# Attention with a normalised output, then a gated convolution network: whole-batch loads, quadrant matmuls and a norm factor spread through DRAM

## The chip, the cores and the metric

The kernel runs on one core of one Trainium2 chip. The metric is the device time of one execution in microseconds, as the median of repeated runs. The engines named below are TensorE (PE, with its weight loads shown apart as PEld), VectorE (DVE), ScalarE (ACT), GpSimd (POOL) and SyncE (SP); transfers run on 16 DMA engines, and in the kernel before all of them are issued from POOL.

## The reference

```
kv  = einsum('bhsd,bhse->bhde', k, v)          # B=8, H=8, S=576, D=64
o   = einsum('bhsd,bhde->bhse', q, kv)
rms = sqrt(mean(o*o, axis=-1) + 1e-6)
x   = (o / rms * g_norm)  -> (B, S, H*D = 512)
h   = relu(x @ w_in)                           # 512 -> 1024
c   = conv_w[0]*h[s-1] + conv_w[1]*h[s] + conv_w[2]*h[s+1]
out = (h * sigmoid(c)) @ w_out                 # 1024 -> 512, float32
```

All inputs are float32 in DRAM; both kernels compute in bfloat16 on the PE and accumulate in float32.

## The kernel before

The attention part runs per batch and per pair of heads (8 x 4 = 32 passes). A pass loads its own slices of k, v and q with nine DMAs from POOL, which also cast to bfloat16 (L163 to L179). The rows they fetch are 64 numbers long. Ten matmuls build the two 64x64 products k'v (L187), and ACT copies them into a block-diagonal 128x128 tile (L191). Five PE transposes turn q (L196), each copied out by ACT (L198). The 576 positions are then treated as a piece of 512 and a piece of 64: the product q*kv (L202), its square on ACT (L205), a matmul with a block of ones that sums the squares over each head and spreads the sum over the head's 64 rows (L208), Ln and Exp on ACT for the inverse root (L211, L213), and one DVE operation that multiplies the product, still in PSUM, by the factor and by `g_norm` into `xT` (L216). Each of these PSUM tiles has one buffer, so the next piece's L202 waits for L216.

The feed-forward part runs per batch. For each of 8 blocks of 128 of the 1024 inner features: matmuls with `w_in` (L230), Relu on ACT (L236), and three DVE operations for the three taps (L240, L241, L245). Then one Sigmoid over the whole batch (L251), one DVE product (L252), 40 matmuls with `w_out` (L257), five DVE copies out of PSUM (L264) and five output DMAs from POOL (L265).

A scheduler in the framework orders each engine's instructions, so the attention of later batches stands between the feed-forward work of earlier ones; within an engine the order is then fixed, and an instruction that waits holds up all that follow on its engine. ACT has one table of functions loaded at a time, and the compiler puts an ACT_TABLE_LOAD wherever the next function is not in it. The weights come first of all on POOL's queue, the 24 small columns of `conv_w` among them (L125), and only then the first batch's k and v.

## Time and profile before

| | |
|---|---|
| time, median of 3 runs | 528.26 us (525.47 to 528.58) |
| span of the profiled execution | 525.6 us |
| ACT busy | 376.4 us (72%) |
| PE busy | 296.3 us (56%), pipelined matmuls with modelled ends |
| POOL busy | 245.9 us (47%) |
| DVE busy | 203.6 us (39%) |
| DMA queue of POOL | 120192 packets, 27.82 MB, 50.0% of 16 engines' span |

The profile is one execution. Busy time counts the stretch in which an engine has an instruction in work. The chain of waits follows the work that ended last back through what released it. The granted TensorE clock is given as a share of 2.4 GHz and stands at 1.00 or 0.50 in any short stretch, so a mean between them is a mixture.

### The profile page before, as it was taken

The numbers are of one execution on the slowest core, as the hardware profiler recorded it, in microseconds if no ns is written. First come the engines' busy times: TensorE is split into PE (matmuls) and PEld (weight loads), VectorE is DVE, ScalarE is ACT, GpSimd is POOL, SyncE is SP. The second block draws the span as 40 slices with busy tenths as digits, with TensorE's granted clock in tenths as the row PEclk, the third lists the DMA queues.
The fourth block names the chain that finished last, engine by engine and source line by source line (L and its number), as shares of the span: only waits on it lengthen the run. The fifth ranks groups of instructions, "written<-read, shape, count | busy, mean of one in ns | idle before, by whom it ended". The sixth has DMA issues, their size and how long they took to land.

```text
span 525.6 us, 4567 instructions
## 1 busy us (share of the span) xinstructions
PE 296.3 (56%) x1414; PEld 129.9 (25%) x1440; DVE 203.6 (39%) x321; ACT 376.4 (72%) x687; POOL 245.9 (47%) x372
## 2 busy tenths in 40 slices
PE   0033346653766663676646756676655765686816
PEld 0011123321322321232212323232222222232302
DVE  4000103442215545223443344523434325768652
ACT  0028888789898888888898779977899788525130
POOL 7999854455676542665435554465533000020202
...
GB/s 305 15 68 70 65 36 34 34 41 40 46 60 98 47 35 23 66 68 60 32 34 56 75 64 35 22 69 81 54 22 24 60 30 2 0 91 1 90 0 90
DMA packets 120216, 28.11 MB, mean 53 GB/s; under 512 B 116864, under 2 KB 116864, under 8 KB 120192
## 3 DMA queue, kind: packets, MB, share of 16 engines
q0 software_dynamic: 120192, 27.82, 50.0%
...
## 4 chain that ended last, share of the span: by engine, by line
ACT 57%; PE 18%; issue 14%; POOL 5%; DVE 3%; DMA 2%; POOLq 0%
ACT L213 15%; ACT L211 14%; PE o_psum L257 6%; ACT rms_sb L211 6%; PE h_psum L230 5%; ACT rms_sb L213 5%; ACT conv_all L251 5%; ACT qT_sb L198 4%; ACT h_all L236 3%; PE ot_psum L202 3%; PE qT_psum L196 2%; POOL conv_w L125 2%; ACT sq_sb L205 2%; DVE xT L216 2%; ACT kv_sb L191 2%
## 5 line engine op out<-in xcount | busy, mean ns | idle before, releaser
L230 PE MATMUL h_psum<-xT,w_in 128*128 128x64 bf16 (+1 forms) x497 | 118.8, 372 | 39.7 <-ACT h_all L236 38.3
L216 DVE SCALAR_TENSOR_TENSOR xT<-ot_psum,g_norm_sbuf,rms_sb 128x512 bf16<-128x512 f32 x64 | 33.1, 517 | 224.1 <-ACT rms_sb L213 224.1
L257 PE MATMUL o_psum<-w_out,hg_all 128*128 128x512 bf16 (+1 forms) x309 | 101.5, 461 | 14.0 <-DVE hg_all L252 13.2
L163 POOL DMA_DIRECT2D k_sb<-in_k_dram x64 | 48.2, 757 | 110.2 <-PE qT_psum L196 77.6
L196 PE MATMUL qT_psum<-ident,q_sb 128*128 128x128 bf16 (+1 forms) x160 | 41.7, 260 | 77.5 <-ACT qT_sb L198 74.1
L213 ACT ACT_TABLE_LOAD x64 | 82.1, 1283 | 1.1
L211 ACT ACT_TABLE_LOAD x64 | 82.1, 1283 | 1.1
L236 ACT ACTIVATE h_all<-h_psum 128x512 bf16<-128x512 f32 (+1 forms) x128 | 48.4, 407 | 41.8 <-PE h_psum L230 38.7
L265 POOL DMA_DIRECT2D out_dram<-o_sb x40 | 22.9, 576 | 115.3 <-DVE o_sb L264 110.4
L230 PEld LDWEIGHTS <-w_in 128*128 128x128 bf16 x512 | 43.8, 118 | 111.0 <-issue 101.7
L174 POOL DMA_DIRECT2D q_sb<-in_q_dram x64 | 49.4, 782 | 46.3 <-PE qT_psum L196 33.8
L187 PE MATMUL kv_psum<-v_sb,k_sb 128*64 128x64 bf16 (+1 forms) x320 | 35.2, 230 | 56.2 <-DMA v_sb<-in_v_dram 31.2
L257 PEld LDWEIGHTS <-hg_all 128*128 128x128 bf16 (+1 forms) x320 | 32.5, 114 | 93.2 <-issue 46.6
L198 ACT ACTIVATE qT_sb<-qT_psum 128x128 bf16<-128x128 bf16 (+1 forms) x160 | 41.9, 262 | 16.5 <-PE qT_psum L196 14.2
L245 DVE SCALAR_TENSOR_TENSOR conv_all<-h_all,conv_w,conv_all 128x575 bf16<-128x575 bf16 x64 | 51.2, 815 | 0.7
L241 DVE SCALAR_TENSOR_TENSOR conv_all<-h_all,conv_w,conv_all 128x575 bf16<-128x575 bf16 x64 | 51.1, 813 | 0.9
L205 ACT ACTIVATE sq_sb<-ot_psum 128x512 bf16<-128x512 f32 x64 | 26.2, 409 | 34.4 <-PE ot_psum L202 32.1
L187 PEld LDWEIGHTS <-k_sb 128*64 128x64 bf16 (+1 forms) x320 | 26.5, 131 | 92.6 <-issue 59.2
L163 POOL DMA_DIRECT2D v_sb<-in_v_dram x64 | 48.2, 758 | 0.3 <-issue 0.2
L264 DVE COPY o_sb<-o_psum 128x512 f32<-128x512 f32 (+1 forms) x40 | 27.5, 688 | 51.9 <-PE o_psum L257 43.6
L202 PE MATMUL ot_psum<-qT_sb,kv_sb 128*128 128x512 bf16 x64 | 25.6, 401 | 22.0 <-DVE xT L216 21.2
L191 ACT ACTIVATE kv_sb<-kv_psum 64x64 bf16<-64x64 f32 x64 | 13.6, 212 | 30.5 <-PE kv_psum L187 29.7
...
## 6 DMA issues: line engine op xcount, KB each, us to landing
out_dram<-o_sb POOLq DMA_DIRECT2D x32, 256.0 KB, 2.4
k_sb<-in_k_dram POOLq DMA_DIRECT2D x64, 64.0 KB, 2.8
v_sb<-in_v_dram POOLq DMA_DIRECT2D x64, 64.0 KB, 2.8
q_sb<-in_q_dram POOLq DMA_DIRECT2D x64, 64.0 KB, 2.7
...
w_out_tmp<-in_moe_w_out_dram POOLq DMA_DIRECT2D x8, 256.0 KB, 6.7
...
```

Source lines behind the costliest of these rows:

```text
L163: nc.gpsimd.dma_start(out=dst[:, :nfull, r], in_=src[b, h0 + hi, :nfull * P, :].rearrange("(p si) d -> p si d", si=nfull, p=P),)
L174: nc.gpsimd.dma_start(out=q_sb[:, :nfull, r], in_=q[b, h0 + hi, :nfull * P, :].rearrange("(si p) d -> p si d", si=nfull, p=P),)
L187: nc.tensor.matmul(kv_psum[r, r], k_sb[:sc, si, r], v_sb[:sc, si, r], start=(si == 0), stop=(si == len(s_chunks) - 1),)
L196: nc.tensor.transpose(qT_psum[:, :sc], q_sb[:sc, si, :], ident128[:sc, :sc])
L198: nc.scalar.activation(qT_sb[:, s0:s0 + sc], qT_psum[:, :sc], AX.Copy)
L211: nc.scalar.activation(rms_sb[:, :nc_], sos_psum[:, :nc_], AX.Ln, bias=eps_sbuf, scale=1.0 / D)
L213: nc.scalar.activation(rms_sb[:, :nc_], rms_sb[:, :nc_], AX.Exp, scale=-0.5)
L230: nc.tensor.matmul(h_psum[:, :], w_in_tiles[ki][:, fi * P:(fi + 1) * P], x_T[ki][:, n0:n0 + nc_], start=(ki == 0), stop=(ki == n_hd - 1),)
L236: nc.scalar.activation(h_sb[:, n0:n0 + nc_], h_psum, AX.Relu)
L241: nc.vector.scalar_tensor_tensor(conv_sb[:, 1:S], h_sb[:, 0:S - 1], cw[:, 0:1], conv_sb[:, 1:S], op0=AL.mult, op1=AL.add,)
L245: nc.vector.scalar_tensor_tensor(conv_sb[:, 0:S - 1], h_sb[:, 1:S], cw[:, 2:3], conv_sb[:, 0:S - 1], op0=AL.mult, op1=AL.add,)
L257: nc.tensor.matmul(o_psum[:sc, :], hg_all[:, fi, s0:s0 + sc], w_out_tiles[fi], start=(fi == 0), stop=(fi == n_ff - 1),)
```

## The change

The file is written anew around the same mathematics.

**Loads.** k, v and q of one whole batch are loaded with one casting DMA each from POOL (batch 0 in two halves). A row is now 6 consecutive positions of one head, 384 numbers (1536 bytes in DRAM). Output DMAs, `w_in`, `g_norm` and `conv_w` go through SP; `conv_w` comes in one DMA and is turned by one PE transpose; `g_norm` is folded into `w_in`.

**Attention.** Positions are kept in the order of residue modulo 6, in two halves ("parities") of 288. A transpose turns 128 columns (two residues of one head), so even residues land on partitions 0 to 63 and odd ones on 64 to 127; DVE copies 576 columns at once (L214). The product q*kv is four matmuls on the four 64x64 quadrants of the array, two heads by two parities, 288 columns each (L267). It is computed twice: once for the squares (L222), and again when the factor is there (L279). Sums of squares of a whole group of batches gather in one PSUM tile of 128 rows (L231); one Ln and one Exp per group (L246, L247) give all factors, which SP writes to DRAM (L249) and reads back with eight broadcasting DMAs, each into 64 partitions (L254).

**Feed-forward.** Chunks of 288 or 384 columns in place of 512 and 64. A tap is one DVE multiplication per tap and feature block (L311, three in place of one) and six additions per two blocks (L315, L316), all bfloat16; Sigmoid and product go over two blocks at once. Output copies are two thirds on ACT, one third on DVE.

**Order.** The batches form five groups, (0), (1,2), (3,4), (5,6), (7). In each stage `interleave` mixes the first feed-forward half of group s, the second half of group s-1 and the attention of group s+1, by weights. The framework's scheduler then orders each engine.

```diff
+GROUPS = ((0,), (1, 2), (3, 4), (5, 6), (7,))
...
+                nc.gpsimd.dma_start(
+                    out=qkv[name, b][:, i * hs:(i + 1) * hs, :],
+                    in_=src[b, i * hs:(i + 1) * hs].rearrange("h (p r) d -> p h (r d)", r=R),
                 )
...
+        def kv_unit(bi, b):
+            k_sb, v_sb = qkv["k", b], qkv["v", b]
+            ps = ps_kq.tile([P, n_hd, D], FP32, name="kv_ps", tag="kq")
+            for hp in range(n_hd):
+                for r in range(R):
+                    for i in range(2):
+                        nc.tensor.matmul(
+                            ps[i * D:(i + 1) * D, hp, :],
+                            k_sb[:, 2 * hp + i, r * D:(r + 1) * D],
+                            v_sb[:, 2 * hp + i, r * D:(r + 1) * D],
+                            start=(r == 0), stop=(r == R - 1))
...
+        def sq_unit(bi, t):
+            ps = out_mm(g, bi, t)
+            sq = attn.tile([P, 2, HS], BF16, name="sq", bufs=5)
+            nc.scalar.activation(sq, ps[:, :, :HS], AX.Square)
...
+        def norm_unit():
+            rs = attn.tile([P, HS], FP32, name="rs")
+            nc.scalar.preload_act_table_set("natural_log_exp_and_others")
+            nc.scalar.activation(rs, g.ss, AX.Ln, bias=eps_sb, scale=1.0 / D)
+            nc.scalar.activation(rs, rs, AX.Exp, scale=-0.5)
+            scr = dram.tile([P, HS], FP32, name="scr")
+            nc.sync.dma_start(out=scr, in_=rs)
+            g.rb = bcast.tile([P, n_hd, 2 * g.G, HS], FP32, name="rb", padded_shape=[P, n_hd, 4, HS])
+            for t in range(n_hd):
+                row = scr[t * SM:t * SM + 4 * g.G, :].rearrange("(c i) n -> i c n", i=2)
+                for i in range(2):
+                    nc.sync.dma_start(
+                        out=g.rb[i * D:(i + 1) * D, t, :, :],
+                        in_=row[i:i + 1].to_broadcast([D, 2 * g.G, HS]))
...
+        ps = ps_ot.tile([P, 2, 512], FP32, name="ot_ps")
+        for i in range(2):
+            for e in range(2):
+                es = slice(e * D, (e + 1) * D)
+                nc.tensor.matmul(
+                    ps[i * D:(i + 1) * D, e, :HS],
+                    g.kv[bi][es, t, i, :], g.qT[bi][es, 2 * t + i, :],
+                    start=True, stop=True)
...
+        def x_unit(bi, t):
+            ps = out_mm(g, bi, t)
+            nc.vector.tensor_mul(
+                g.xT[:, t, bi * S:(bi + 1) * S].rearrange("p (e n) -> p e n", n=HS),
+                ps[:, :, :HS], g.rb[:, t, 2 * bi:2 * bi + 2, :])
...
+                for j in range(3):
+                    col = j * n_ff + f0 + f
+                    nc.vector.tensor_scalar_mul(taps[j][:, f, :], g.h[:, f0 + f, :], cw[:, col:col + 1])
+            v = [t.rearrange("p f (b n) -> p (f b) n", n=S) for t in taps]
+            for at, n, prev in NEIGHBOURS:
+                here, there = slice(at, at + n), slice(prev, prev + n)
+                nc.vector.tensor_add(v[1][:, :, here], v[1][:, :, here], v[0][:, :, there])
+                nc.vector.tensor_add(v[1][:, :, there], v[1][:, :, there], v[2][:, :, here])
+            nc.scalar.activation(taps[1], taps[1], AX.Sigmoid)
...
+    for s in range(ng + 1):
+        a = []
+        if s + 1 < ng:
+            for b in (groups[s + 2].bs if s + 2 < ng else ()):
+                load(b)
+            a = attn_a(groups[s + 1]) + [(4.0, lambda: None)] + attn_b(groups[s + 1])
+        m1 = mm1(groups[s]) if s < ng else []
+        m2 = mm2(groups[s - 1]) if s > 0 else []
+        interleave(m1, m2, a)
```

On ACT, in the first pass of the kernel before (`rms_sb` is the factor, `qT_sb` and `sq_sb` as above; L211 and L213 are Ln and Exp):

```order
L205 ACTIVATE sq_sb<-ot_psum 128x512
L211 ACT_TABLE_LOAD
L211 ACTIVATE rms_sb<-sos_psum,eps_sbuf 128x512
L213 ACT_TABLE_LOAD
L213 ACTIVATE rms_sb<-rms_sb 128x512
L198 ACTIVATE qT_sb<-qT_psum 128x128 x3
L205 ACTIVATE sq_sb<-ot_psum 128x64
```

On ACT of the changed kernel, in the stage that runs the feed-forward of batches 1 and 2 and the attention of batches 3 and 4 (`rs` is the factor of the group, `h` the Relu output, `tap_` the convolution sum that Sigmoid takes):

```order
L317 ACTIVATE tap_1150<-tap_1150 128x2304
L246 ACT_TABLE_LOAD
L246 ACTIVATE rs<-ss_ps,eps_sb 128x288
L303 ACTIVATE h<-h_ps 128x384
L247 ACT_TABLE_LOAD
L247 ACTIVATE rs<-rs 128x288
L303 ACTIVATE h<-h_ps 128x384 x6
L317 ACT_TABLE_LOAD
```

Before, a pair of table loads stands at each of 64 pieces; now one Ln and one Exp serve a group, with three loads around them, and 15 loads stand in the whole program.

On SP of the changed kernel, for the same group (`scr` is the DRAM tile, `rb` the spread factor, `out_dram` the output):

```order
L350 DMA out_dram<-o_sb 32x512
L249 DMA scr<-rs 128x288
L350 DMA out_dram<-o_sb 64x512 x2
L254 DMA rb<-scr 64x4x288 x8
L350 DMA out_dram<-o_sb 32x512
L350 DMA out_dram<-o_sb 96x512 x2
```

Before, SP issues nothing and the factor never leaves SBUF; now a write and eight reads stand between the Exp and its use, and outputs queue with them.

On DVE of the changed kernel, at the first use of a spread factor by this group (`xT<-ot_ps,rb` is the product of L279; the `tap_` and `h` rows are the convolution of batches 1 and 2):

```order
L315 TENSOR_TENSOR tap_1396<-tap_1396,tap_1395 128x4x288
L316 TENSOR_TENSOR tap_1396<-tap_1396,tap_1397 128x4x288
L319 TENSOR_TENSOR h<-h,tap_1283 128x2304
L279 TENSOR_TENSOR xT<-ot_ps,rb 128x576
L315 TENSOR_TENSOR tap_1396<-tap_1396,tap_1395 128x4x192
L316 TENSOR_TENSOR tap_1396<-tap_1396,tap_1397 128x4x192
```

On DVE before, `xT` (L216) waits for ACT alone; now the first L279 of a group waits for DMAs, in the middle of the last convolution unit of the group before it, whose remaining additions stand behind it.

On PE before, ahead of the first sum of squares (`sos_psum`); the `kv_psum` rows belong to the next pair of heads:

```order
L202 MATMUL ot_psum<-qT_sb,kv_sb 128x512
L187 LDWEIGHTS k_sb
L187 MATMUL kv_psum<-v_sb,k_sb 64x64
L230 LDWEIGHTS w_in_84
L230 MATMUL h_psum<-xT_0_178,w_in_84 128x64
L187 LDWEIGHTS k_sb
L187 MATMUL kv_psum<-v_sb,k_sb 64x64
L208 LDWEIGHTS ones_165
L208 MATMUL sos_psum<-sq_sb,ones_165 128x512
```

On PE of the changed kernel, ahead of the first norm (`ss_ps` gathers the squares of batch 0, `kv_ps` is the k'v product of batch 1):

```order
L231 MATMUL ss_ps<-sq,sel 32x288
L191 LDWEIGHTS k_sb
L191 MATMUL kv_ps<-v_sb,k_sb 64x64
...
L191 MATMUL kv_ps<-v_sb,k_sb 64x64
L231 LDWEIGHTS sel
L231 MATMUL ss_ps<-sq,sel 32x288
```

Before, two matmuls of the next pair of heads stand between a product and its sum; now the last five matmuls of batch 0's sum stand behind 39 matmuls of batch 1's k'v, and so behind the loads of the whole of batch 1's k and v.

## Rows read from the trace of the kernel before

**Rows 1.** The page, part 1: busy us (share of the span) and instructions.

```profile
span 525.6 us, 4567 instructions
...
PE 296.3 (56%) x1414; PEld 129.9 (25%) x1440; DVE 203.6 (39%) x321; ACT 376.4 (72%) x687; POOL 245.9 (47%) x372
```

**Rows 2.** The page, part 4: the chain that ended last, by engine and by line.

```profile
ACT 57%; PE 18%; issue 14%; POOL 5%; DVE 3%; DMA 2%; POOLq 0%
ACT L213 15%; ACT L211 14%; PE o_psum L257 6%; ACT rms_sb L211 6%; PE h_psum L230 5%; ACT rms_sb L213 5%; ACT conv_all L251 5%; ACT qT_sb L198 4%; ACT h_all L236 3%; PE ot_psum L202 3%; PE qT_psum L196 2%; POOL conv_w L125 2%; ACT sq_sb L205 2%; DVE xT L216 2%; ACT kv_sb L191 2%
```

**Rows 3.** Groups by line and shape, ACT: count, busy us, mean ns, idle before.

```profile
L211 ACT ACT_TABLE_LOAD x64 | 82.1, 1283 | 1.1
L213 ACT ACT_TABLE_LOAD x64 | 82.1, 1283 | 1.1
L236 ACT ACTIVATE h_all<-h_psum 128x512 bf16<-128x512 f32 x64 | 38.0, 594 | 20.7 <-PE h_psum L230 17.6 <-PE sos_psum L208 1.9 <-PE ot_psum L202 1.1
...
L251 ACT ACTIVATE conv_all<-conv_all 128x4608 bf16<-128x4608 bf16 x8 | 32.3, 4043 | 3.0 <-DVE conv_all L245 2.9
L211 ACT ACTIVATE rms_sb<-sos_psum,eps_sbuf 128x512 f32<-128x512 f32 x32 | 22.0, 687 | 0.5
...
L236 ACT ACTIVATE h_all<-h_psum 128x64 bf16<-128x64 f32 x64 | 14.1, 220 | 21.1 <-PE h_psum L230 21.1
```

**Rows 4.** Groups by line and shape, DVE.

```profile
L245 DVE SCALAR_TENSOR_TENSOR conv_all<-h_all,conv_w,conv_all 128x575 bf16<-128x575 bf16 x64 | 51.2, 815 | 0.7
...
L216 DVE SCALAR_TENSOR_TENSOR xT<-ot_psum,g_norm_sbuf,rms_sb 128x512 bf16<-128x512 f32 x32 | 24.0, 750 | 117.2 <-ACT rms_sb L213 117.1
L240 DVE TENSOR_SCALAR conv_all<-h_all,conv_w 128x576 bf16<-128x576 bf16 x64 | 22.9, 370 | 4.8 <-ACT h_all L236 4.4
L264 DVE COPY o_sb<-o_psum 128x512 f32<-128x512 f32 x32 | 22.1, 689 | 45.1 <-PE o_psum L257 36.7 <-remote 5.9 <-DMA k_sb<-in_k_dram 1.5
L252 DVE TENSOR_TENSOR hg_all<-h_all,conv_all 128x4608 bf16<-128x4608 bf16 x8 | 20.5, 2558 | 26.8 <-ACT conv_all L251 26.8
...
L119 DVE CAST w_out<-w_out_tmp 128x512 bf16<-128x512 f32 x8 | 3.4, 427 | 1.8 <-DMA w_out_tmp<-in_moe_w_out_dram 1.8
L112 DVE CAST w_in<-w_in_tmp 128x1024 bf16<-128x1024 f32 x4 | 2.8, 694 | 6.0 <-DMA w_in_tmp<-in_moe_w_in_dram 6.0
```

**Rows 5.** Windows: us, busy of PE, PEld, DVE, ACT, POOL, clock, DMA share, GB/s.

```profile
36.00:468.00 432.00, 260.52 (x1236) 113.94 (x1259) 162.76 (x255) 357.94 (x657) 208.82 (x304) 0.72 0.54 48
380.00:390.00 10.00, 7.74 (x36) 3.42 (x36) 5.02 (x8) 8.35 (x18) 4.24 (x6) 0.50 0.47 30
455.60:459.00 3.40, 3.35 (x8) 1.19 (x9) 1.91 (x3) 0.43 (x1) 0.00 (x0) 0.50 0.00 0
462.00:466.20 4.20, 4.15 (x20) 1.68 (x18) 1.38 (x2) 0.00 (x0) 1.61 (x3) 1.00 0.34 132
```

**Rows 6.** Timeline, PE, k'v matmuls: start us, us, [idle before].

```profile
30.36 0.37 PE L187 MATMUL kv_psum<-v_sb,k_sb 128*64 128x64 bf16 x4 [30.36 <-DMA v_sb<-in_v_dram]
...
66.06 0.61 PE L187 MATMUL kv_psum<-v_sb,k_sb 128*64 128x64 bf16 x5
```

**Rows 7.** Groups by line and shape, PE: matmuls of 128 and 64 columns.

```profile
L196 PE MATMUL qT_psum<-ident,q_sb 128*128 128x128 bf16 x128 | 34.5, 269 | 73.7 <-ACT qT_sb L198 70.3 <-DMA q_sb<-in_q_dram 3.2
...
L187 PE MATMUL kv_psum<-v_sb,k_sb 128*64 128x64 bf16 x256 | 23.7, 226 | 55.4 <-DMA v_sb<-in_v_dram 30.4 <-ACT kv_sb L191 23.3 <-DMA q_sb<-in_q_dram 1.5
```

**Rows 8.** The page, parts 2, 3 and 6: rate per slice, queue, issues (us to landing).

```profile
GB/s 305 15 68 70 65 36 34 34 41 40 46 60 98 47 35 23 66 68 60 32 34 56 75 64 35 22 69 81 54 22 24 60 30 2 0 91 1 90 0 90
...
q0 software_dynamic: 120192, 27.82, 50.0%
...
out_dram<-o_sb POOLq DMA_DIRECT2D x32, 256.0 KB, 2.4
k_sb<-in_k_dram POOLq DMA_DIRECT2D x64, 64.0 KB, 2.8
```

More of the change, by code (lines that the diff above doesn't have):

```diff
@@ L55, with interleave @@
 AL = mybir.AluOpType
+PSUM = bass.MemoryType.PSUM
+DRAM = bass.MemoryType.DRAM
+GROUPS = ((0,), (1, 2), (3, 4), (5, 6), (7,))
+def interleave(*lists):
+    keyed = []
+    for n, units in enumerate(lists):
+        total = float(sum(w for w, _ in units)) or 1.0
+        at = 0.0
+        for m, (w, fn) in enumerate(units):
+            keyed.append(((at + 0.5 * w) / total, n, m, fn))
+            at += w
+    for _, _, _, fn in sorted(keyed, key=lambda x: x[:3]):
+        fn()
 @with_exitstack
@@ new lines @@
+    SM = 32
+    pool = lambda name, bufs, **kw: ctx.enter_context(tc.tile_pool(name=name, bufs=bufs, **kw))
+    consts = pool("consts", 1)
+    loads = pool("loads", 2)
+    attn = pool("attn", 2)
+    big = pool("big", 2)
+    bcast = pool("bcast", 1)
+    conv = pool("conv", 2)
+    outp = pool("outp", 3)
+    dram = pool("dram", 2, space=DRAM)
+    ps_h = pool("ps_h", 2, space=PSUM)
+    ps_o = pool("ps_o", 2, space=PSUM)
+    ps_ot = pool("ps_ot", 1, space=PSUM)
+    ps_ss = pool("ps_ss", 1, space=PSUM)
@@ new lines @@
+    ps_kq = pool("ps_kq", 1, space=PSUM)
+    from concourse.masks import make_identity
+    ident = consts.tile([P, P], BF16, name="ident")
+    make_identity(nc, ident)
+    ident32 = consts.tile([3 * n_ff, 3 * n_ff], FP32, name="ident32")
+    make_identity(nc, ident32)
+    eps_sb = consts.tile([P, 1], FP32, name="eps_sb")
+    nc.vector.memset(eps_sb, eps)
+    sel = consts.tile([P, 4, SM], BF16, name="sel")
+    nc.vector.memset(sel, 0.0)
+    for c in range(4):
+        nc.vector.memset(sel[:D, c, 2 * c:2 * c + 1], 1.0)
+        nc.vector.memset(sel[D:, c, 2 * c + 1:2 * c + 2], 1.0)
@@ L168, with load @@
+    qkv = {}
+    def load(b, parts=1):
+        hs = H // parts
+        for i in range(parts):
+            for name, src in (("k", k), ("v", v), ("q", q)):
+                if i == 0:
+                    qkv[name, b] = loads.tile([PS, H, R * D], BF16, name=name + "_sb")
                 nc.gpsimd.dma_start(
-                    out=dst[:sc, nfull, :].rearrange("p (h d) -> p h d", h=2, d=D),
-                    in_=src[b, h0:h0 + 2, s0:s0 + sc, :].rearrange("h p d -> p h d"),
-                )
@@ L172 @@
-            for hi in range(2):
-                r = slice(hi * D, hi * D + D)
-                nc.gpsimd.dma_start(
-                    out=q_sb[:, :nfull, r],
-                    in_=q[b, h0 + hi, :nfull * P, :].rearrange(
-                        "(si p) d -> p si d", si=nfull, p=P),
-                )
-            nc.gpsimd.dma_start(
-                out=q_sb[:sc, nfull, :].rearrange("p (h d) -> p h d", h=2, d=D),
-                in_=q[b, h0:h0 + 2, s0:s0 + sc, :].rearrange("h p d -> p h d"),
-            )
@@ L183 @@
-            kv_psum = attn_psum.tile([P, P], FP32, name="kv_psum")
-            for hi in range(2):
-                r = slice(hi * D, hi * D + D)
-                for si, (s0, sc) in enumerate(s_chunks):
-                    nc.tensor.matmul(
-                        kv_psum[r, r], k_sb[:sc, si, r], v_sb[:sc, si, r],
-                        start=(si == 0), stop=(si == len(s_chunks) - 1),
-                    )
-                nc.scalar.activation(kv_sb[r, r], kv_psum[r, r], AX.Copy)
-            qT_sb = attn.tile([P, S], BF16, name="qT_sb")
@@ new lines @@
+    w_stage = []
+    for t in range(n_hd):
+        st = loads.tile([P, D_ff], FP32, name="w_stage")
+        nc.sync.dma_start(out=st, in_=moe_w_in[t * P:(t + 1) * P, :])
+        nc.vector.tensor_scalar_mul(w_in_sb[:, t, :], st, g_sb[:, 0:1])
+    cw_ps = ps_ss.tile([P, 3 * n_ff], FP32, name="cw_ps", tag="ss")
+    nc.tensor.transpose(cw_ps, cw_rows, ident32)
+    cw = consts.tile([P, 3 * n_ff], FP32, name="cw")
+    nc.vector.tensor_copy(cw, cw_ps)
+    load(1)
+    w_out_sb = consts.tile([P, n_ff, D_model], BF16, name="w_out_sb")
```

271 lines of the change are left out of this document (128 added, 143 removed).

## The prediction

> **What bounds the kernel now.** I read the page's engine shares first, then the chain that ended last, then the groups by line and shape, and last a few windows and the timeline. The shares [rows 1] put ACT in front with 376.4 us of 525.6; PE is 120 us behind by pipelined, modelled busy time, DVE has 203.6. The chain [rows 2] is 57% ACT, and its two largest lines, L213 and L211 with 15% and 14%, are not Exp and Ln but the table loads ahead of them: 64 each, 1283 ns every time [rows 3], 164.2 us together. From 36 to 468 us ACT is busy 357.94 of 432 us [rows 5], 83%, at a mean PE clock of 0.72: a kernel bound by one engine, with some loss at hand-overs. The first matmul waits for v until 30.36 us [rows 6], because POOL issues the weights first.
>
> **The sum, engine by engine.** The rewrite leaves little in place, so I price each engine's whole new work from rows, then the start, the end and the loss between them.
>
> ACT. Relu costs 594 ns for 512 columns and 220 for 64 [rows 3], so 0.835 ns a column: 72 of 384 columns at 0.49 and 32 of 288 at 0.41 make 48 us. 32 squares of 576 at 0.65: 21. Sigmoid at 4043/4608 = 0.877 ns a column: 12 of 2304 and 8 of 1152, 35. 32 copies of k'v (256 columns) at 0.38: 12. 25 output copies at 0.594: 15. Five Ln and Exp of 288 at up to 0.5 each: 5. Table loads stand 15 times in the new order, 19 us, for the 128 of those two rows. Together 155 us, so 221 of 376 go, 145 of them table loads.
>
> DVE. The fixed part of an operation comes from the casts, 427 ns for 512 and 694 for 1024 [rows 4]: 0.16 us, and 0.52 ns a column. The three taps were 0.37 + 0.81 + 0.82 us for 576 columns (L240 and the two shifted ones, of which L245 is shown). A tap is now a multiplication like L240: 48 of 576 at 0.37, and 72 of 1152, unseen, between 0.37 (nothing for the second half) and 0.67 (0.37 plus 576 columns at the cast's rate); I take 0.55, from 0.16 fixed and the rest in proportion, so 57 us (44 to 66). Additions at the rate of L252 (2558 ns for 4608): 48 in the one-batch groups and 72 in the two-batch ones, of 576, 384, 190 and of 1152, 768, 380 columns, 58 us; if the shifted third runs at half that rate, 6 more. Products with h: 22. Products with the spread factor: L216's 750 ns stretched to 576 columns, 0.82, 32 times, 26. Copies of transposed q: between a cast from SBUF (0.46 for 576) and a copy out of PSUM (689 ns for 512, so 0.76); I take 0.76 as it reads PSUM, 24 (15 to 24). Output copies 12 at 0.69: 8. Weights and memsets: 4. Together 200 us (178 to 212), about what DVE does now, but in place of 39% of the span it must fit into far less.
>
> PE. At clock 1.00, 20 matmuls of 512 columns take 4.15 us [rows 5], 0.21 each; at 0.50, 8 take 3.35. The feed-forward is 288 matmuls of 384 and 128 of 288 columns (60 us) and 296 of 512 (62). k'v: 384 matmuls of 64 columns, between their streaming time at the first rate (0.03) and 0.61/5 = 0.12 [rows 6]; I take 0.06, 23 us (12 to 46). 192 transposes of 96 columns: between 0.04 streaming and an isolated 0.269 [rows 7], at which they no longer run since six go in a row; I take 0.08, 15 us (8 to 52). q*kv twice: 256 matmuls of 288 columns, 0.118 each if one after another, 30 us; if four quadrants run at once, 8; I take 20. Sums of squares: 64 likewise, 5 (2 to 8). The new order changes the shape of the used array 191 times (133 before). A change can cost nothing, or up to what an isolated 64-column matmul lasts above its spacing, 0.226 - 0.06 = 0.17 us [rows 7]: 0 to 32 us, I take 16. Together 201 us at clock 1.00 (about 152 to 290 at the ends).
>
> The Trainium skill, TensorEngine Tiling (Array Packing), section Key Properties, says that tiles work independently and in parallel, and that a change of tiling mode drains the engine. By its first half the quadrant products are 8 us and not 20; by its second every one of the 191 changes is paid, 32 and not 16; PE would be 205 us. No row before shows a 64x64 quadrant, so neither half can be read there.
>
> So three engines stand at 200, 201 and 155 us, where one stood at 376.
>
> **The start.** Batch 0's k, v and q (3.54 MB of float32) and `w_in` (2.10 MB) come first, 5.64 MB at the 305 GB/s of the first slice [rows 8]: 18.5 us. By the order of PE the first norm stands behind 39 matmuls of batch 1's k'v, 2.36 MB more: 26 us. Sum, table load (1.28), Ln and Exp: 29. The spread: a write, 2.4 us from issue to landing [rows 8], and eight reads that fill 1.18 MB; POOL's queue has batch 1's q, `w_out` and batch 2 in flight, so I give the reads half the rate, 7.7 us, and 2.4 for the landing: 41 us. Four products with the factor, each a PE visit and 0.82 on DVE, about 3 to 4 us: **44 us** until the feed-forward runs freely. By then DVE has done 13 of its 200 us (weights, eight copies of q, four products), PE about 20 of 201.
>
> **The middle and the end.** 187 us are left on DVE and 181 on PE. With two engines even, neither runs without holes: a product with the factor sits in DVE's queue with convolution work behind it, the PSUM tile of q*kv has one buffer, and so has the one shared by k'v and the transposes. I take the share that ACT reached as the bound, 0.83 [rows 5]: 187/0.83 = **225 us**. It is the weakest number here: one bound engine gave it, and two even ones could do worse, while the interleaving by weights could do better. After DVE's last product come the rest of five output tiles of 8 matmuls (two can start early; some 6 us), a copy (0.69) and a landing (2.3): **9 us**. 44 + 225 + 9 = 278. The profiled execution, at 525.6 us, lies 0.5% under the median of 528.26, so **280 us**.
>
> What is hidden: POOL's issues. They were 757 ns each or less for up to 512 packets and number 28 now; loads of a group are queued one stage ahead. If that cover is gone (a transfer takes longer than a stage), the rival on packets below applies. The second q*kv is 10 of PE's 201 us.
>
> **Rivals.**
> *The spread is exposed each time (0.12).* After the Exp of each of the four later groups come a table load, a write and eight reads of up to 2.36 MB: 1.3 + 2.4 + 7.7 + 2.4, 14 us, with outputs in the same SP queue. For it: the L279 rows stand within the convolution's queue on DVE, so a late factor holds both. Against: some ten DVE operations and a row of Relus lie between Exp and first use. If all four are bare, 280 + 4 x 12 = **328 us**.
> *Casting loads cost by the byte (0.08).* A packet takes 0.50 x 16 x 525.6/120192 = 35 ns [rows 1, 8], with 256 bytes read. The new ones read 1536. At a price by the byte, 18432 packets x 0.21 us/16 = 242 us of all engines, and outputs, spread and weights (23 MB at 305 GB/s) 75 more: the queue bounds, and with the last stage behind it **340 us**. For it: the rate of these loads never passes 98 GB/s. Against: POOL's issues alone explain that.
> *The clock stays low (0.07).* In 380 to 390 us it is 0.50 with PE busy 7.74 of 10 [rows 5]. If PE is held at the lower level throughout, its 122 us of feed-forward double and small matmuls grow by a third or so: 122 + 25 more, 44 + (181 + 147)/0.9 + 9 = **417 us**. Against: between 462 and 466, with PE never idle, it is 1.00, and the new PE order offers other work at most waits.
> *Everything overlaps (0.10).* DVE at its lower price and 0.9: 44 + 165/0.9 + 9 = **236 us**.
> *The broadcast reads serialise (0.02), the other side.* 64 partitions read the same DRAM row, 8192 packets of 1152 bytes in all. If these were served one at a time, at 305/16 = 19 GB/s, 60 ns each, that is 492 us in the path between each group's Exp and its products, with about 155 us that cannot lie beside it (start, attention, last stages): **647 us**. It is slower than before only from 45 ns a packet, (528 - 155)/8192. No row shows such a read.
> That the change doesn't do what it says is settled for the table loads by the order.
>
> **How the numbers follow.** The likeliest case, three engines at a moderate loss, has 0.60, and 255 to 310 as its own range (a share between 0.92 and 0.73). 0.01 is left for about no change by mishaps I can't name. The range takes in the low end of the overlap case and reaches into packets and spread: **245 to 335**, leaving out about half of the first of these, the upper half of the packet case, the clock and the serialised reads, some 0.2. A difference of 1% is about what a measurement of this kernel can tell from none. Faster by over 1%: **0.97**; within: **0.01**; slower: **0.02**.
>
> **What would show it.** Right: 15 table loads, ACT near 155 us; DVE near 200 with L311 of 1152 columns at 0.55; first L300 matmuls about 40 us; PE clock mostly 1.00 after that. A chain with DVE and PE shares in place of ACT's 57%. Wrong: DVE's L279 waiting on `rb` for over 10 us per group (spread); PE waiting on `k_sb`, `v_sb` or `q_sb` after the first 30 us (packets); a clock under 0.7 in dense stretches; k'v or transposes above 0.12 us each.

## The result, and the profile after

The changed kernel takes 272.92 us (270.27 to 273.57, 4 runs) against 527.24 us for the kernel before beside it: a ratio of 0.517 (95% interval 0.514 to 0.520). 280.0 us was forecast, 2.6% more. The profiled execution spans 268.2 us.

The page, part 1 (busy us, share of the span, instructions) and part 4 (the chain that ended last, by engine and by line), of the changed kernel:

```profile
span 268.2 us, 4181 instructions
...
PE 200.9 (75%) x1609; PEld 101.6 (38%) x1609; DVE 162.9 (61%) x351; ACT 146.1 (54%) x238; POOL 22.0 (8%) x36
...
PE 42%; ACT 22%; DMA 14%; DVE 13%; issue 4%; SPq 3%; POOL 1%; DVEq 0%; POOLq 0%; ACTq 0%
PE h_ps L300 18%; PE o_ps L336 14%; ACT tap L317 8%; DMA rb<-scr 7%; DMA v_sb<-in_v_dram 5%; PE ot_ps L267 4%; ACT h L303 3%; DVE xT L279 3%; PE qT_ps L211 3%; SPq L254 3%; DVE tap L311 2%; PE ss_ps L231 2%; DVE h L319 2%; ACT L317 2%; ACT L247 2%
```

ACT's 376.4 [rows 1] are 146.1, and no engine holds the chain as ACT's 57% did [rows 2]. Groups by line and shape (count, busy us, mean ns, idle before and what ended it):

```profile
L311 DVE TENSOR_SCALAR tap<-h,cw 128x1152 bf16<-128x1152 bf16 x72 | 33.0, 512 | 8.5 <-ACT h L303 8.4
L279 DVE TENSOR_TENSOR xT<-ot_ps,rb 128x576 bf16<-128x576 f32 x32 | 24.1, 754 | 25.4 <-DMA rb<-scr 17.7 <-PE ot_ps L267 7.6
L214 DVE COPY qT<-qT_ps 128x576 bf16<-128x576 bf16 x32 | 14.6, 455 | 22.5 <-PE qT_ps L211 22.3
L341 DVE COPY o_sb<-o_ps 128x512 f32<-128x512 f32 x12 | 8.3, 689 | 6.8 <-PE o_ps L336 6.6
L317 ACT ACT_TABLE_LOAD x6 | 7.7, 1283 | 0.1
L246 ACT ACT_TABLE_LOAD x4 | 5.1, 1283 | 0.1
L247 ACT ACT_TABLE_LOAD x4 | 5.1, 1283 | 0.1
```

With the first load (L245) that makes the 15 table loads that the order showed, where 128 stood in two rows [rows 3]. Windows (us, busy of PE, PEld, DVE, ACT, POOL, clock, DMA share, GB/s) show where no engine is full:

```profile
30.00:40.00 10.00, 2.56 (x24) 2.05 (x24) 1.83 (x4) 0.31 (x1) 1.25 (x2) 1.00 1.27 220
70.00:80.00 10.00, 5.30 (x65) 3.31 (x65) 4.94 (x14) 5.17 (x9) 0.77 (x1) 0.66 0.92 170
80.00:90.00 10.00, 7.50 (x61) 3.80 (x60) 3.46 (x7) 1.51 (x4) 1.55 (x2) 0.83 1.16 239
120.00:140.00 20.00, 11.63 (x81) 5.76 (x78) 17.98 (x33) 12.32 (x15) 0.00 (x0) 0.83 0.57 126
140.00:170.00 30.00, 30.00 (x193) 13.13 (x192) 20.52 (x39) 21.22 (x34) 0.00 (x0) 1.00 0.23 63
170.00:190.00 20.00, 13.34 (x118) 7.02 (x117) 15.53 (x29) 11.37 (x18) 0.00 (x0) 0.87 0.67 152
```

From 140 to 170 us PE never stops. Around 35, from 70 to 90, 120 to 140 and 170 to 190 it does, for 7.4 + 7.2 + 8.4 + 6.7 us, and the granted clock falls there from the second of these on. These stretches lie near the first products of groups 0 to 3, but not all of this is waiting for a factor. In the stretch from 120 us PE's longest wait is for DVE's product `h`, while DVE is busy 17.98 of the 20 us:

```profile
132.20 0.61 PE L336 MATMUL o_ps<-w_out_sb,h 128*128 128x512 bf16 x1 [5.15 <-DVE h L319]
```

The chain of waits at group 1 (start us, us, what):

```profile
67.80 1.28 ACT L247
69.10 0.44 ACT rs L247
...
79.14 1.70 SPq L254
80.84 0.04 issue
80.88 13.02 DMA rb<-scr
93.90 0.03 DVEq L279
93.94 0.04 issue
93.98 0.77 DVE xT L279
```

From the end of Exp at 69.5 us to the landing of the last piece of the factor 24.4 us go by. The write has landed at 75.1, SP begins to issue the last of the eight reads at 80.9, this one lands 13 us later, and the DMA engines are shared with the loads of batches 5 and 6. The chain has no feed-forward matmul in this time.

**A table by stages.** To compare kernels I read the end of each group's last product (L279) from the timeline and take differences. The pieces of a row add up to the span:

| kernel | to g0 | g0 to g1 | g1 to g2 | g2 to g3 | g3 to g4 | rest | span |
|---|---|---|---|---|---|---|---|
| changed kernel | 47.4 | 53.0 | 47.5 | 49.0 | 31.9 | 39.4 | 268.2 |
| a_spread_out | 34.1 | 31.0 | 42.3 | 46.1 | 38.3 | 41.0 | 232.8 |
| a_loads_few | 47.6 | 48.7 | 47.4 | 48.8 | 31.9 | 39.4 | 263.8 |
| a_no_tables | 48.5 | 44.0 | 46.0 | 46.1 | 31.2 | 40.3 | 256.1 |
| a_dve_less | 49.3 | 54.1 | 49.4 | 46.5 | 32.2 | 38.2 | 269.7 |
| a_pe_less | 47.6 | 52.1 | 51.6 | 48.0 | 32.5 | 38.5 | 270.3 |
| a_gap12 | 48.0 | 48.3 | 47.2 | 45.1 | 35.3 | 41.3 | 265.2 |
| a_mix | 36.1 | 43.3 | 49.7 | 47.7 | 35.4 | 41.3 | 253.5 |
| a_mix_newton | 38.4 | 44.7 | 51.3 | 48.4 | 33.9 | 40.9 | 257.6 |

The rows below the first are experiments. Wherever a row's time fell by more than 2%, most of it fell in the first two columns.

### The profile page after: what moved, and what is told of

It is laid out like the page before. It is cut to its first block, busy times and chain, and to the rows that moved or that the text cites. A ratio compares the mean times of both kernels' runs of the same rounds, so it can differ in the third digit from the quotient of the medians.

```text
span 268.2 us, 4181 instructions
## 1 busy us (share of the span) xinstructions
PE 200.9 (75%) x1609; PEld 101.6 (38%) x1609; DVE 162.9 (61%) x351; ACT 146.1 (54%) x238; POOL 22.0 (8%) x36
## 3 DMA queue, kind: packets, MB, share of 16 engines
q0 software_dynamic: 19904, 15.21, 37.2%
## 4 chain that ended last, share of the span: by engine, by line
PE 42%; ACT 22%; DMA 14%; DVE 13%; issue 4%; SPq 3%; POOL 1%; DVEq 0%; POOLq 0%; ACTq 0%
PE h_ps L300 18%; PE o_ps L336 14%; ACT tap L317 8%; DMA rb<-scr 7%; DMA v_sb<-in_v_dram 5%; PE ot_ps L267 4%; ACT h L303 3%; DVE xT L279 3%; PE qT_ps L211 3%; SPq L254 3%; DVE tap L311 2%; PE ss_ps L231 2%; DVE h L319 2%; ACT L317 2%; ACT L247 2%
## 5 line engine op out<-in xcount | busy, mean ns | idle before, releaser
L336 PE MATMUL o_ps<-w_out_sb,h 128*128 128x512 bf16 (+1 forms) x296 | 78.3, 399 | 13.3 <-DVE h L319 12.0
L300 PE MATMUL h_ps<-xT,w_in_sb 128*128 128x384 bf16 (+1 forms) x416 | 82.7, 324 | 6.3 <-ACT h L303 5.8
L303 ACT ACTIVATE h<-h_ps 128x384 bf16<-128x384 f32 (+1 forms) x104 | 46.7, 464 | 25.4 <-PE h_ps L300 24.8
L311 DVE TENSOR_SCALAR tap<-h,cw 128x1152 bf16<-128x1152 bf16 (+1 forms) x120 | 47.8, 452 | 15.6 <-ACT h L303 15.4
L300 PEld LDWEIGHTS <-w_in_sb 128*128 128x128 bf16 x416 | 37.6, 99 | 37.0 <-issue 13.0
L336 PEld LDWEIGHTS <-h 128*128 128x128 bf16 (+1 forms) x296 | 28.3, 101 | 45.2 <-DVE h L319 14.8
L317 ACT ACTIVATE tap<-tap 128x2304 bf16<-128x2304 bf16 (+1 forms) x20 | 34.8, 1738 | 13.9 <-DVE tap L316 13.9
L279 DVE TENSOR_TENSOR xT<-ot_ps,rb 128x576 bf16<-128x576 f32 x32 | 24.1, 754 | 25.4 <-DMA rb<-scr 17.7
L200 ACT ACTIVATE kv_sb<-kv_ps 64x256 bf16<-64x256 f32 x32 | 12.1, 377 | 45.1 <-PE kv_ps L191 44.8
L267 PE MATMUL ot_ps<-qT,kv_sb 64*64 64x288 bf16 x256 | 23.0, 338 | 14.7 <-DVE xT L279 14.4
L319 DVE TENSOR_TENSOR h<-h,tap 128x2304 bf16<-128x2304 bf16 (+1 forms) x20 | 22.3, 1116 | 15.6 <-ACT tap L317 15.5
L214 DVE COPY qT<-qT_ps 128x576 bf16<-128x576 bf16 x32 | 14.6, 455 | 22.5 <-PE qT_ps L211 22.3
L211 PE MATMUL qT_ps<-ident,q_sb 96*128 96x96 bf16 x192 | 18.6, 250 | 12.3 <-DVE qT L214 6.7
L316 DVE TENSOR_TENSOR tap<-tap,tap 128x1152 bf16<-128x1152 bf16 (+5 forms) x60 | 26.9, 471 | 0.0
L315 DVE TENSOR_TENSOR tap<-tap,tap 128x1152 bf16<-128x1152 bf16 (+5 forms) x60 | 26.8, 469 | 0.0
L222 ACT ACTIVATE sq<-ot_ps 128x576 bf16<-128x576 f32 x32 | 20.9, 652 | 5.5 <-PE ot_ps L267 5.4
L211 PEld LDWEIGHTS <-q_sb 96*128 96x128 bf16 x192 | 15.3, 123 | 19.7 <-issue 18.3
L267 PEld LDWEIGHTS <-kv_sb 64*64 64x64 bf16 x256 | 9.1, 108 | 32.7 <-issue 30.5
L191 PE MATMUL kv_ps<-v_sb,k_sb 96*64 96x64 bf16 x384 | 11.9, 218 | 10.5 <-DMA v_sb<-in_v_dram 10.5
## 6 DMA issues: line engine op xcount, KB each, us to landing
k_sb<-in_k_dram POOLq DMA_DIRECT2D x7, 576.0 KB, 12.1
v_sb<-in_v_dram POOLq DMA_DIRECT2D x7, 576.0 KB, 15.6
q_sb<-in_q_dram POOLq DMA_DIRECT2D x7, 576.0 KB, 12.7
```

What stands on the lines that cost most here:

```text
L191: nc.tensor.matmul(ps[i * D:(i + 1) * D, hp, :], k_sb[:, 2 * hp + i, r * D:(r + 1) * D], v_sb[:, 2 * hp + i, r * D:(r + 1) * D], start=(r ...
L211: nc.tensor.transpose(ps[:, i, j * PS:(j + 1) * PS], q_sb[:, 2 * hp + i, j * P:(j + 1) * P], ident[:PS, :PS])
L267: nc.tensor.matmul(ps[i * D:(i + 1) * D, e, :HS], g.kv[bi][es, t, i, :], g.qT[bi][es, 2 * t + i, :], start=True, stop=True)
L279: nc.vector.tensor_mul(g.xT[:, t, bi * S:(bi + 1) * S].rearrange("p (e n) -> p e n", n=HS), ps[:, :, :HS], g.rb[:, t, 2 * bi:2 * bi + 2, :])
L300: nc.tensor.matmul(ps, w_in_sb[:, t, f * P:(f + 1) * P], g.xT[:, t, cs], start=(t == 0), stop=(t == n_hd - 1))
L303: nc.scalar.activation(g.h[:, f, cs], ps, AX.Relu)
```

## The experiments

Theory A, with which I began: three engines of 146 to 201 us, and the loss spread over all hand-overs, as the prediction's share of 0.83 has it. B: the loss sits where products wait for the factor that goes through DRAM. C: that wait is long because batch loads share the DMA engines. The other experiments price table loads, DVE and PE.

**The factor's way through DRAM taken out** (a_spread_out).

```diff
-            g.rb = bcast.tile(...)
-            for t in range(n_hd):
-                ...   # eight reads of scr
+            g.rb = rb_const   # all ones, set once
```

> The changed kernel with the products taking a constant tile in place of the spread factor: norm, Ln, Exp and the write to DRAM stay, the forty reads and every wait for them go; the output lacks the normalisation. Theory A (three engines near 160 to 200 us of work, loss spread over all hand-overs): only the start improves, about 12 us (first product at 29 instead of 42.7), and what the holes give back is lost again at the next hand-over; 255 to 262 us. Theory B (the loss sits where a group's products wait for the spread): PE's idle time in 30-40, 70-100, 120-140 and 170-190 (7.4 + 8.8 + 8.4 + 6.7 = 31 us) comes back, with the one before g4 some 35: 235 to 242 us.

Measured: 234.55 us (0.445 of before, 0.442 to 0.447), 38.4 less than the changed kernel.

```profile
PE 188.2 (81%) x1589; PEld 98.0 (42%) x1609; DVE 165.4 (71%) x352; ACT 145.8 (63%) x238; POOL 22.9 (10%) x36
```

The engines' work is the same as before the edit, so the 38 us hang on the factor's way: B, not A. Not all of them were idle time. Of the 35.4 us between the two spans 22.7 are PE's idle time and 12.7 its busy time, which is shorter for the same matmuls at a mean clock of 0.984 in place of 0.946. The edit also frees SP's queue and the DMA engines of the reads, which this run does not tell from the wait itself. The table of stages is sharper than the theory was: 13.3 us came in front of group 0's last product and 22.0 in the stage to group 1; the next two stages gave 8.1, the last one took back 6.4 and the rest 1.6. In the later stages the feed-forward of two batches stands beside the spread; at groups 0 and 1 there is none or that of one batch.

**The loads of batches 3 to 7 taken out** (a_loads_few).

```diff
-                load(b)
+                for name in ("k", "v", "q"):
+                    qkv[name, b] = qkv[name, 1 + (b - 1) % 2]
```

> The changed kernel with batches 3 to 7 computed from the tiles of batches 1 and 2: fifteen loads of q, k and v (17.7 MB read) go, all arithmetic stays; the output is that of the wrong inputs for five batches. Theory C (group 1's spread is late because its reads share the DMA engines with the loads of batches 2 to 4): reads of rb land in 5 to 7 us everywhere, not 13; Exp of group 1 to its first product falls from 24 to about 10 us; 258 to 263 us. Theory A or B without C: under 4 us, 269 to 273 us, since the later spreads, at 120 and 170 us, had no loads beside them.

Measured: 265.73 us (0.503, 0.501 to 0.505), 7.2 less, between the two ranges. C holds for one place: the stage to group 1 shortens by 4.3 us, the others by 0.3 at most. There the last piece of the factor lands 15.5 us after Exp in place of 24.4, but Exp to last product falls only from 30.9 to 27.0 us. (The 24 us of the expectation are the way to that landing; the first product follows Exp after 10.8 us, and after 7.0 here.) The time between spans (4.4 us) is smaller than that between medians (7.2), so a part of this I can't place. 4 to 7 us against the 38 of the whole wait: sharing the DMA engines is a minor part of it.

**The table loads around the norm taken out** (a_no_tables).

```diff
-            nc.scalar.preload_act_table_set("natural_log_exp_and_others")
-            nc.scalar.activation(rs, g.ss, AX.Ln, bias=eps_sb, scale=1.0 / D)
-            nc.scalar.activation(rs, rs, AX.Exp, scale=-0.5)
+            nc.scalar.activation(rs, g.ss, AX.Square, scale=1.0 / D)
+            nc.scalar.activation(rs, rs, AX.Square, scale=-0.5)
```

> The changed kernel with Ln and Exp replaced by Square: same instructions and waits, 2 table loads in place of 15, so ACT loses 13 x 1.283 = 16.7 us; the output has a wrong factor. If ACT were on the path throughout: 256 us. Theory A: ACT (146 of 268 us) has room, but two loads lie in each norm's path, 5 x 1.3 to 2.6 = 6 to 13 us at most, part of it covered: 262 to 268 us. Theory B: the norm's path is the bare one, all of these count: 258 to 262 us.

Measured: 259.45 us (0.493, 0.491 to 0.496), 13.5 less for 16.7 us of loads. That is near the price of an engine that is always on the path, though ACT is busy 54% of the span: the loads stand in the norm's path. 9.0 of the 12.1 us by the spans fall in the stage to group 1. There, in the changed kernel, a Sigmoid stands between Ln and Exp on ACT, so that three loads (63.5, 65.3 and 67.8 us) lie between the sum and the factor. Without them the factor is there 4.3 us earlier (65.3 in place of 69.5 us); why its way to the last product is 3.7 us shorter as well, this run does not show.

**Work taken from DVE** (a_dve_less; a_so_dve_less is the same on top of a_spread_out).

```diff
...
-                for j in range(3):
+                for j in (1, 2):
...
-                nc.vector.tensor_add(v[1][:, :, here], v[1][:, :, here], v[0][:, :, there])
```

> The changed kernel without the first tap: 40 multiplications and 60 additions of DVE go, about 16 + 27 = 43 of its 163 us; the convolution has two of its three taps. As the prediction put it (DVE bounds the middle with a share of 0.83): 43/0.83 = 52 us less, 221 us. Theory A (PE at 201 us is next to it): 12 to 20 us less, 253 to 261 us. Theory B (the holes at the spreads and PE's own work make up the time, DVE matters only where it holds a product back): 3 to 10 us less, 263 to 270 us.

> a_spread_out without the first tap too (two of three taps, a constant factor): DVE falls from 165 to about 122 us at an unchanged PE of 188. If PE is the bound once no product waits: 226 to 234 us, no more than 4% under a_spread_out. If DVE bounds the middle as the prediction put it and the spread only hid this: 43/0.83 = 52 us at most, 190 to 205 us.

Measured: 271.03 us (0.513, 0.510 to 0.516), some 2 less, hardly clear of noise and just above B's range, and 229.4 us (0.435, 0.433 to 0.437), 5.2 less than a_spread_out. The pages of a_dve_less and of a_so_dve_less:

```profile
PE 200.3 (74%) x1594; PEld 102.0 (38%) x1609; DVE 128.0 (47%) x251; ACT 145.4 (54%) x238; POOL 22.2 (8%) x36
```

```profile
PE 188.6 (83%) x1589; PEld 97.7 (43%) x1609; DVE 130.3 (58%) x252; ACT 144.5 (64%) x237; POOL 22.5 (10%) x36
```

DVE lost 35 us of busy time in each (45.5 in a_dve_less by single durations, which overlap) and the time did not follow. DVE bounds the kernel neither with the waits nor without them.

**Work taken from PE** (a_pe_less).

```diff
-            for t in range(n_hd):
+            for t in range(n_hd - 1):
...
-                    start=(t == 0), stop=(t == n_hd - 1))
+                    start=(t == 0), stop=(t == n_hd - 2))
```

> The changed kernel with three of four matmuls of the first projection: 104 matmuls of PE go, 72 x 0.162 + 32 x 0.122 = 15.6 us of 201; a quarter of the sum over the model dimension is left out. If PE is what the time outside the holes follows: 12 to 17 us less, 256 to 261 us. If the time follows DVE, ACT and the hand-overs: under 5 us, 268 to 273 us. The kernel without 43 us of DVE's work lost 2 us.

Measured: 272.34 us (0.515, 0.513 to 0.518), 0.6 less, within the measurement. But PE did not become 15.6 us shorter. Its page and the largest of its matmul groups, with the same group of the changed kernel below them:

```profile
PE 197.6 (73%) x1489; PEld 95.2 (35%) x1505; DVE 162.4 (60%) x351; ACT 145.7 (54%) x238; POOL 22.0 (8%) x36
...
L336 PE MATMUL o_ps<-w_out_sb,h 128*128 128x512 bf16 x264 | 76.0, 425 | 21.1 <-DVE h L319 17.7 <-ACT o_sb L343 2.4 <-issue 0.4
```

```profile
L336 PE MATMUL o_ps<-w_out_sb,h 128*128 128x512 bf16 x280 | 74.4, 400 | 13.3 <-DVE h L319 12.0 <-ACT o_sb L343 0.9 <-DVE o_sb L341 0.4
```

The mean granted clock fell from 0.946 to 0.872, the `w_out` matmuls took 425 ns in place of 400, and PE's busy time sank by 3.3 us, not 15.6. Windows of a_pe_less in which PE is not full and the clock is low:

```profile
120.00:130.00 10.00, 4.75 (x19) 2.11 (x19) 8.27 (x15) 9.49 (x13) 0.00 (x0) 0.62 0.32 79
130.00:140.00 10.00, 6.82 (x36) 3.29 (x38) 7.31 (x12) 2.87 (x3) 0.00 (x0) 0.50 0.81 173
180.00:190.00 10.00, 5.98 (x42) 3.23 (x40) 8.53 (x16) 2.48 (x2) 0.00 (x0) 0.52 0.74 160
```

So the time does not follow the number of PE's matmuls here. Whether the clock took the gain, or fell because PE waited for something else anyway, this run does not separate.

**The products placed later** (a_gap12, a_gap30).

```diff
-            a = attn_a(groups[s + 1]) + [(4.0, lambda: None)] + attn_b(groups[s + 1])
+            a = attn_a(groups[s + 1]) + [(12.0, lambda: None)] + attn_b(groups[s + 1])
```

> The changed kernel with one number changed: the gap that the interleaving leaves between a group's norm and its products weighs 12 in place of 4, so that the norm stands at 44% of a stage and not at 65%, and more feed-forward matmuls stand between it and the first product. B1 (the wait for the spread is only exposed because the product stands too early in PE's queue): the holes at 120-140 and 170-190 (8.4 + 6.7 us) and the one before the last group close, group 1's closes in part since its stage is short: 246 to 256 us. B2 (the feed-forward work that could stand there is itself held by DVE, ACT or the group before): 263 to 275 us.

> As a_gap12 with a weight of 30: the attention of the next group stands in the first quarter of a stage. B1: no more than a_gap12 gives, 243 to 256 us, since its gap should already cover 9 us. If the loads of a group come too late for an attention so early, PE waits for v_sb or k_sb in the stages of groups 2 and 3 and the time is 5 to 15 us above a_gap12's.

Measured: 268.36 us (0.509, 0.506 to 0.511) and 268.39 us (0.511, 0.508 to 0.514), some 4.5 less each. B1 fell as a forecast of time, for both gaps. With the gap of 12 the Exps of groups 2 to 4 ended 8 to 9 us earlier (115.1, 162.5, 203.8 in place of 123.5, 170.7, 212.4) and the stage to group 3 became 3.9 us shorter, but the stage to group 4 and the rest gave 5.3 back. What was won lies in the stage to group 1, 4.7 us shorter. 2.1 of them are a table load: a Relu and not a Sigmoid stands there between Ln and Exp, and Exp ends at 67.4 in place of 69.5 us. That stage has only one batch's feed-forward to put behind the spread. Together with a_spread_out this says that the spreads of groups 2 to 4 were never the main loss.

**The factor spread by TensorE** (a_pe_spread for all groups; a_mix for groups 0 and 1, the others through DRAM with the gap of 12; the gap ahead of group 1's products stays 4).

```diff
...
+                ps = pool_.tile([P, HS], FP32, name="rb_ps", tag=tag)
+                nc.tensor.matmul(
+                    ps, selT[t * SM:(t + 1) * SM, c, :], g.rs16[t * SM:(t + 1) * SM, :],
+                    start=True, stop=True)
+                nc.scalar.activation(g.rb[:, t, c, :], ps, AX.Copy)
...
```

> The changed kernel with the factor spread by TensorE: Exp writes bf16, 64 matmuls of 32 rows by 128 columns and 288 elements with a 0/1 matrix put it into PSUM, 64 ACT copies of 288 columns (0.41 us) take it to SBUF; the write and the forty reads go. PE gains 64 x 0.12 = 8 us, ACT 26 us (to 172). Theory B: the spread takes about 3 us after Exp in place of 8 to 24, so 234.6 us (the kernel without any wait for the factor) + 8 of PE + 2 to 3 per norm: 245 to 257 us. Theory A: the added 34 us of work eat what the wait gives, 265 to 275 us.

> The changed kernel with the factor of groups 0 and 1 spread by TensorE, that of groups 2 to 4 through DRAM with the gap of 12. Theory B' (the spread through DRAM costs time only where no feed-forward work stands behind it, at groups 0 and 1: there the last product moved from 47.4 to 34.1 and from 100.4 to 65.1 us without it, 13 + 22 us, while groups 2 to 4 together added 3): 268.4 (the gap of 12 alone) less 12 and 18 to 22, plus 3 to 5 us of added PE work: 236 to 245 us. If instead each spread costs its part, two of five groups give under half of the 38 us: 252 to 262 us, no better than the spread by TensorE everywhere (259.4).

Measured: 259.41 us (0.492, 0.489 to 0.494), between the two ranges, and 254.90 us (0.483, 0.481 to 0.485). a_mix is the fastest kernel here that leaves nothing out, 6.6% under the changed kernel. Its time lies in the range that I gave to the other theory, but the table of stages does not: against a_gap12 it gained 11.9 us in front of group 0, 5.0 in the stage to group 1 (9.7 against the changed kernel, which has the same gap there), and nothing after (from there on it lost 5.2). So the place was right and the price of the substitute wrong. Windows of a_mix behind the norm of group 1:

```profile
60.00:70.00 10.00, 6.30 (x25) 1.50 (x25) 4.93 (x13) 8.05 (x16) 0.00 (x0) 0.70 0.05 7
70.00:80.00 10.00, 9.17 (x85) 3.77 (x86) 5.00 (x7) 6.08 (x13) 0.63 (x1) 0.50 0.10 27
```

First products follow Exp by 1.2 and 1.5 us there (11.8 and 10.8 in the changed kernel). But the stage to group 1 is 43.3 us, between 53.0 (through DRAM) and 31.0 (no factor): 16 spread matmuls, 16 ACT copies and the products run one after another with PE's clock at the lower of its two levels, 0.50, in 70 to 80 us, though PE is busy 9.17 of 10.

**The inverse root on DVE** (a_mix_newton).

```diff
...
-            nc.scalar.activation(rs, g.ss, AX.Ln, bias=eps_sb, scale=1.0 / D)
...
-                nc.scalar.activation(g.rs16, rs, AX.Exp, scale=-0.5)
...
+            nc.vector.tensor_scalar(out=ms, in0=g.ss, scalar1=1.0 / D, scalar2=eps, op0=AL.mult, op1=AL.add)
...
+            nc.vector.tensor_scalar(out=sh, in0=ms.bitcast(I32), scalar1=1, scalar2=None, op0=AL.logical_shift_right)
+            nc.vector.tensor_scalar(out=rs.bitcast(I32), in0=sh, scalar1=-1, scalar2=0x5f3759df, op0=AL.mult, op1=AL.add)
...
+            for it in range(2):
+                nc.vector.tensor_mul(tmp, rs, rs)
+                nc.vector.scalar_tensor_tensor(tmp, tmp, -0.5, ms, op0=AL.mult, op1=AL.mult)
+                nc.vector.scalar_tensor_tensor(out16 if it else rs, tmp, 1.5, rs, op0=AL.add, op1=AL.mult)
```

> a_mix with the factor's inverse root computed on DVE in place of Ln and Exp on ACT: a shift and a subtraction on the integer bits as a first guess and two Newton steps, nine operations of 288 columns (0.35 to 0.45 us each, 16 to 20 us of DVE in all), and 13 table loads (16.7 us) and ten activations (4.7 us) less on ACT. If the table loads' price of 13.5 us is still to be had once the spread of the first two groups is off the path, and DVE's work is as cheap as the 2 us for 43 us say: 239 to 246 us. If the norm's path is only traded (3.5 us on DVE, in its queue, for two loads and two activations on ACT), or DVE becomes the wait: 248 to 258 us.

Measured: 259.77 us (0.490, 0.486 to 0.495), some 4 to 5 above a_mix and above both ranges. One of the three lines of a step, from the tile's view:

```profile
L266 DVE SCALAR_TENSOR_TENSOR tmp<-tmp,ms x10: 448/451/459, 28.9 to 197.5; 128x288 f32<-128x288 f32 x10
```

ACT fell from 157.0 to 135.3 us, DVE rose from 163.2 to 178.7. The nine operations take 4.1 us one behind the other (27.3 to 31.4 us at group 0). Ln and Exp took 0.94, without a load at group 0 and with two or three later. The path of the norm is only traded, and at group 0 made longer: its last product moved from 36.1 to 38.4 us. Together with a_dve_less: 35 us less on DVE outside the norm's path gave 2, some 15 more with part of it inside that path cost 5.

**The table loads of the kernel before taken out** (b_exp_square, an edit of the kernel before).

```diff
-                nc.scalar.activation(rms_sb[:, :nc_], rms_sb[:, :nc_], AX.Exp, scale=-0.5)
+                nc.scalar.activation(rms_sb[:, :nc_], rms_sb[:, :nc_], AX.Square, scale=-0.5)
```

> The kernel before with Square in place of Exp, in the table set of the function ahead of it: 13 table loads in place of 135, 122 x 1.283 = 156.5 us of ACT's 376; the factor is wrong. If ACT is the path in full, as the prediction has it for its 64 + 64 loads: 527 - 157 = 370 us, at the share of 0.83 even 338. If PE with its clock at 0.72 in the middle, or the chain of hand-overs of a pair of heads, is next behind ACT: 400 to 450 us, and more of the gain to 273 us comes from the other parts of the rewrite.

Measured: 376.97 us (0.714 of before, 0.712 to 0.716), 151 less for 156.5 us of loads.

```profile
PE 243.7 (65%) x1414; PEld 112.3 (30%) x1440; DVE 204.5 (55%) x321; ACT 214.5 (57%) x565; POOL 245.8 (66%) x372
```

The chain of rows 2 told the truth, nearly us for us: of the change's 254 us, 151 (59%) were to be had by this alone. PE's busy time fell with it from 296.3 [rows 1] to 243.7 us for the same matmuls, at a mean clock of 0.89. Which parts of the rewrite gave the other 103 us, no run here separates.

## Why the prediction was right, and where it was not

**Right: what bounded the kernel, and most of the start.** ACT came to 146.1 us against 155 forecast; its single durations, which is what the forecast adds up, come to 154.8. The 155 held a small slip: Sigmoid at its 0.877 ns a column makes 32 us and not 35, and 34.8 were measured. Three readings in the prediction were off without consequence: PE was 80 us behind ACT and not 120, POOL's issues for q took 782 ns where it has 757 at most, and by its own rule the tap of 1152 columns is 0.58 us and not 0.55. Exp of group 0 ends at 28.9 us (29 forecast) and the first product begins at 40.6 (41). The steps between are partly luck: the sum of squares came about 2 us later than the 26, and the table load of 1.28 us was not in the path. The four products took 6.8 us and not 3 to 4, since each waited for its own piece of the factor. The first feed-forward matmul stands at 41.8 us, and these matmuls run freely only from 47.4, where 44 was forecast.

**Wrong by size: DVE's 200 us.** 162.9 were measured. Copies of q took 455 ns, the lower bound, and not 0.76 us (9 us less). The Trainium skill, VectorE: DVE Perf Modes, section Why PSUM operands drop a tier, says that a PSUM operand holds float32 to the lowest rate but lets 16-bit data keep the next one; the rows agree, with 455 ns for 576 bfloat16 columns and 689 ns for 512 float32 ones. Taps of 1152 columns took 512 ns, not 550, and those of 576 362 (3 less in all). Additions came to 56.4 us by single durations, not 58; the shifted third was not slower. All single durations together make 183.9 us, 16 under the forecast. The other 21 us are the ends of operations that overlap the next one, which a sum of durations counts twice.

**Right sum by luck, other make-up: PE's 201 us** (200.9). Timeline of the changed kernel, PE:

```profile
17.60 0.85 PE L191 MATMUL kv_ps<-v_sb,k_sb 96*64 96x64 bf16 x24 [6.17 <-DMA v_sb<-in_v_dram]
...
58.42 0.32 PE L267 MATMUL ot_ps<-qT,kv_sb 64*64 64x288 bf16 x4
58.67 0.30 PE L300 MATMUL h_ps<-xT,w_in_sb 128*128 128x288 bf16 x1
```

The k'v matmuls stand less than 0.03 us apart and keep PE busy for 11.9 us, not 23. Four quadrant matmuls last 0.32 us together, their starts being 3 to 4 ns apart, so the 256 of them are nearer 8 us than my 20. From the last of them to the next start with the full array 239 ns pass, 0.12 of them for its own columns, and most other changes of shape cost 0.09 to 0.12 as well, about 191 x 0.1 = 19 us against the 16 taken. The Trainium skill, TensorEngine Tiling (Array Packing), section Key Properties, says that tiles work in parallel and that a change of mode drains the engine. The trace agrees with the first half by these starts, and with the second as far as a change has a price, nearer 0.1 us than the 0.17 of the prediction's upper end; that the draining is what costs it, no row shows. What brings the sum back to 201 is in part the clock, 0.946 on the mean: a_spread_out has 188.2 us at 0.984 for the same matmuls. The rest I could not place.

**Wrong in mechanism: the middle as 187 us of DVE at a share of 0.83.** This is the step that failed, the one the prediction called its weakest. a_dve_less should have given 52 us by it, and gave 2. With DVE's measured sum the same formula gives 44 + 150/0.83 + 9 = 234 us, 39 too few. The forecast of 280 was near by luck, because two errors offset each other: DVE was over-sized by 37 us (45 at that share), and the waits for the spread factor and the norm, put into the middle only as a general loss, cost about as much (25 of a_spread_out's 38.4 us lie behind the start, and a_no_tables gave 13.5). That 234 is also the time of a_spread_out is in part chance, as a_so_dve_less shows that DVE is not the bound there either.

**The rival that came partly true: the spread exposed each time.** It was priced at 14 us for each of four later groups. The whole wait costs 38.4 us, 13 of which lie in the start, where the forecast had it; 22 lie at group 1, and groups 2 to 4 cost about nothing net. The argument against it (ten DVE operations and a row of Relus stand between Exp and first use) holds for these three, and fails at group 1, where the stage has only one batch's feed-forward and SP's reads meet the loads.

**The other rivals.** Casting loads by the byte: a packet took 0.372 x 16 x 268.2/19904 = 80 ns, between the 35 of before and the 210 of the rival.

```profile
q0 software_dynamic: 19904, 15.21, 37.2%
...
rb<-scr SPq DMA_DIRECT2D x24, 288.0 KB, 6.9
```

PE's waits for `v_sb` are two, both before 18 us; the later loads stay hidden. Serialised broadcast reads: the 256 packets of a read would take 15 us at 60 ns and eight reads 123 us; their median landing is 6.9 us with the eight in flight together, and where no loads run beside them (groups 2 and 3) one lands some 1.28 us after the other. A clock held low throughout did not come, but low stretches did, and in a_pe_less the `w_out` matmuls were slower with them (425 ns in place of 400).

**What stays open.** In the stages of groups 2 to 4 (47.5, 49.0 and 31.9 us) neither 35 us of DVE, nor a quarter of PE's first projection, nor a larger gap moved the time by more than some us. PE waits there for `h` from DVE (8.3 of 12.0 us in all, the second longest of its waits), and in windows with such waits the mean clock is lower (0.83 from 120 to 140 us, 0.87 from 170 to 190). Which of these is first I could not separate.
